# Transposing queries, keys and one-hot rows in larger groups, in a routed attention with a hard-swish FFN

## Chip, cores and metric

The kernel runs on one core of one Trainium2 chip. The metric is the device time of one execution in microseconds (us). Before the change it is 1071.25 us, the median of three runs (1070.79 to 1073.04 us). Engines are called as in the profile: PE is TensorE (PEld is its weight load), DVE is VectorE, ACT is ScalarE, POOL is GpSimd, SP is the engine that issues most DMA. L350 is line 350 of the kernel before.

## What is computed

First an attention in which a query may only look at keys of its own cluster, then a dense FFN. The reference, cut to what matters:

```python
# q, k, v: (4, 8, 768, 64); centroids: (8, 16, 64)
q_assign = np.argmax(np.einsum('bhsd,hcd->bhsc', q_n, c_n), axis=-1)     # q_n, k_n, c_n: unit rows
k_assign = np.argmax(np.einsum('bhsd,hcd->bhsc', k_n, c_n), axis=-1)
mask = q_assign[:, :, :, None] == k_assign[:, :, None, :]
scores = np.where(mask, scale * np.matmul(q, k.transpose(0, 1, 3, 2)), -1e9)
attn = softmax(scores)
x = np.matmul(attn, v)                      # regrouped to (3072, 512)
h = x @ w_in                                # 512 -> 2048
g = h * np.clip(h + 3.0, 0.0, 6.0) / 6.0
out = g @ w_out                             # 2048 -> 512
```

The kernel adds the mask by a second matmul into the same scores: a query's cluster as a one-hot row (1 at its cluster), a key's as the opposite row times a huge negative number (0 at its cluster, -2^60 at the others). Their product is 0 for the same cluster and -2^60 for another.

## The kernel before

Two heads are treated together as a pair; there are 16 pairs, g = 0 to 15. A pair has 12 chunks of 128 rows: 6 of queries (j = 0 to 5) and 6 of keys (j = 6 to 11). Each chunk holds both heads side by side. Before a pair's scores can run, its prep must be done; it is done while the pair before it runs its scores:

```python
NCH, NC2, NHC = 6, 12, 3          # chunks of queries, of both, half of NCH

def scratch(shape, name):         # a PSUM buffer for the prep
    if st["early"]:
        return psum_m.tile(shape, F32, name=name, tag="m")     # 2 buffers, shared with the FFN
    return psum_t.tile(shape, F32, name=name, tag="t")         # 1 buffer

def turn(g, part):                # queries and keys transposed: 4 parts of 3 chunks
    if part == 0:
        st["xf", g] = xp.tile([P, NC2, P], F32, name="xf")
    qk, xf = st["qk", g], st["xf", g]
    pt = scratch([P, NHC, P], "pqk")
    for i in range(NHC):
        j = part * NHC + i
        nc.tensor.transpose(out=pt[:, i], in_=qk[:, j // NCH, j % NCH], identity=ident)   # L294
    dst = xf[:, part * NHC : (part + 1) * NHC]
    nc.scalar.copy(out=dst, in_=pt)                                                       # L296

def cluster_scores(g): ...        # pcs: 4 matmuls of xf with the centroids, copied to cs by ACT
def route(g): ...                 # pr: 3 transposes of cs; DVE makes one_hot (bf16) from them

def route_turn(g, part):          # one-hot rows transposed by a matmul: 3 parts of 4 chunks
    if part == 0:
        st["xm", g] = xp.tile([P, NC2, P], BF16, name="xm")
    xm = st["xm", g]
    po = scratch([P, 4, P], "po")
    for i in range(4):
        j = part * 4 + i
        nc.tensor.matmul(                                                                 # L350
            po[:, i], lhsT=one_hot[:, j], rhs=(ident_q if j < NCH else ident_k),
            start=True, stop=True,
        )
    nc.scalar.copy(out=xm[:, part * 4 : part * 4 + 4], in_=po)                            # L354
```

`ident_k` is the identity times -2^60, so the matmul transposes and scales at once.

```python
def scores(n):                    # one of 12 blocks of a pair: key chunk j against half of the queries
    g, hf, j = where(n)
    scores_qk(n)                  # ps <- xf: key chunk 6 + j against 3 query chunks, both heads (L370)
    scores_part(n, st["xm", g], False)   # ps <- xm: the same with the one-hot rows, added (L370)
    ... ACT: ex = exp(ps)         # L382; ps has 2 buffers
    ... POOL: acc += ex           # L386, L389

def divide(n):                    # every 6 blocks
    pd = scratch([P, 512], "pd")
    ... PE: pd = sums of acc      # L420
    nc.vector.reciprocal(out=rcp, in_=pd)                                                 # L424
    ...

def prep_items(g, r):             # what of pair g's prep is done at which step
    if r in (0, 2):
        return [lambda: turn(g, r), lambda: turn(g, r + 1)]
    return {
        4: [lambda: cluster_scores(g)],
        6: [lambda: route(g)],
        8: [lambda: route_turn(g, 0), lambda: route_turn(g, 1)],
        10: [lambda: route_turn(g, 2)],
    }.get(r, [])

for n in range(0, total + lag_d + 2, 2):        # two blocks in each step; total = 192
    g, r = divmod(n, 12)
    scores(n); scores(n + 1)
    attn_v(n - 2); attn_v(n - 1)                # pv <- ex, vt (L399)
    if (n - 3) % 6 == 5: divide(n - 3)          # so at r = 2 and r = 8
    prep = prep_items(g + 1, r)
    if r == 4: prep.pop()()
    if n == 96: st["early"] = False             # from here on the scratch is the single buffer
    ...
    for i in range(max(len(prep), want)):       # want: how many FFN items this step takes
        if i < want: fill.pop(0)()              # an FFN item: 16 matmuls (ph, X or Y)
        if i < len(prep): prep[i]()
    ... some steps of weight decoding (DVE, ACT), until n = 96
```

In the steps up to n = 54 no FFN item runs, from n = 56 to 94 one in some of the steps, from n = 96 on mostly two or more. The engines execute in the order in which this loop records their instructions. Pair 0's prep runs before the loop (all parts in a row).

Of the kernel before, what the change touches and what calls it, by code (L numbers as in the profile page):

```python
# [8 lines left out]
F32 = mybir.dt.float32  # L9
BF16 = mybir.dt.bfloat16  # L10
# [3 lines left out]
ACT = mybir.ActivationFunctionType  # L14
# [4 lines left out]
P = 128  # L19
NCH = S // P  # L20
NC2 = 2 * NCH
HALF = S // 2
NHC = NCH // 2
# [17 lines left out]
FAR = 2.0**60  # L41
# [75 lines left out]
def fast_path(ctx, tc, ok, q, k, v, centroids, moe_w_in, moe_w_out, out):  # L117
# [3 lines left out]
    nc = tc.nc  # L121
    PSUM = bass.MemoryType.PSUM

    def pool(name, bufs, **kw):
        return ctx.enter_context(tc.tile_pool(name=name, bufs=bufs, **kw))

    const = pool("const", 1)
# [15 lines left out]
    psum_t = pool("psum_t", 1, space=PSUM)  # L143
    psum_m = pool("psum_m", 2, space=PSUM)
# [3 lines left out]
    g_sb = const.tile([P, 7, NFT // 2, P], F32, name="g_sb")  # L148
    ident = const.tile([P, P], F32, name="ident")
    ident_q = const.tile([P, P], BF16, name="ident_q")  # L150
    ident_k = const.tile([P, P], BF16, name="ident_k")
    ones = const.tile([P, D], F32, name="ones")
    half_c = const.tile([P, 1], F32, name="half_c")
    low_c = const.tile([P, 1], F32, name="low_c")
# [1 line left out]
    one_hot = const.tile([P, NC2, P], BF16, name="one_hot")  # L156
# [7 lines left out]
    st = {}  # L164
    later = []

    def scratch(shape, name):

        if st["early"]:
            return psum_m.tile(shape, F32, name=name, tag="m")  # L170
        return psum_t.tile(shape, F32, name=name, tag="t")

# [25 lines left out]
    def load_weights(i):  # L198
        if i < len(chunks):
            st["raw", i] = rawp.tile([P, WC, 2], U32, name="raw")  # L200
            nc.sync.dma_start(st["raw", i], chunks[i][1])
# [54 lines left out]
    def constants():  # L256
        make_identity(nc, ident)
        nc.vector.tensor_copy(out=ident_q, in_=ident)
        nc.vector.tensor_scalar_mul(out=ident_k, in0=ident, scalar1=-FAR)
        for t in range(2):  # L260
            nc.vector.tensor_reduce(
                out=parity[:, t : t + 1],
                in_=ident.rearrange("p (h t c) -> p t h c", t=2, c=C)[:, t], axis=AX.XY, op=ALU.max,
            )
        nc.gpsimd.memset(half_c, 0.5)
        nc.gpsimd.memset(low_c, 1.0 / BOUND)
        nc.gpsimd.memset(ones, 1.0)
        nc.gpsimd.memset(w_low, W_LOW)
        nc.gpsimd.memset(one_hot, 0.0)
# [17 lines left out]
    def turn(g, part):  # L287
        if part == 0:
            st["xf", g] = xp.tile([P, NC2, P], F32, name="xf")
        qk, xf = st["qk", g], st["xf", g]  # L290
        pt = scratch([P, NHC, P], "pqk")
        for i in range(NHC):
            j = part * NHC + i
            nc.tensor.transpose(out=pt[:, i], in_=qk[:, j // NCH, j % NCH], identity=ident)  # L294
        dst = xf[:, part * NHC : (part + 1) * NHC]
        nc.scalar.copy(out=dst, in_=pt)  # L296
        if part == 3:
            st.pop(("qk", g))


# [2 lines left out]
    def cluster_scores(g):  # L303
        c0, xf = (2 * g) % H * C, st["xf", g]
        ps = scratch([P, 512], "pcs")[:, 0 : NC2 // 4 * P]
        for a in range(4):
            nc.tensor.matmul(  # L307
                ps[a * 2 * C : (a + 1) * 2 * C], lhsT=cnT[:, c0 : c0 + 2 * C], rhs=xf[:, a::4],
                start=True, stop=True,
            )  # L310
        cs = st["cs", g] = rtp.tile([P, NC2 // 4, P], F32, name="cs")
        nc.scalar.copy(out=cs, in_=ps)
# [30 lines left out]
    def route_turn(g, part):  # L343
        if part == 0:
            st["xm", g] = xp.tile([P, NC2, P], BF16, name="xm")
        xm = st["xm", g]
        po = scratch([P, 4, P], "po")
        for i in range(4):
            j = part * 4 + i
            nc.tensor.matmul(  # L350
                po[:, i], lhsT=one_hot[:, j], rhs=(ident_q if j < NCH else ident_k),
                start=True, stop=True,
            )
        nc.scalar.copy(out=xm[:, part * 4 : part * 4 + 4], in_=po)  # L354


    def where(n):
# [3 lines left out]
    def scores_qk(n):  # L361
        g, hf, j = where(n)
        st["ps", n] = psum_s.tile([P, 2, 512], F32, name="ps")
        scores_part(n, st["xf", g], True)
# [179 lines left out]
    def prep_items(g, r):  # L544

        if g >= NPAIR:
            return []
        if r in (0, 2):
            return [lambda: turn(g, r), lambda: turn(g, r + 1)]
        return {  # L550
            4: [lambda: cluster_scores(g)],
            6: [lambda: route(g)],
            8: [lambda: route_turn(g, 0), lambda: route_turn(g, 1)],
            10: [lambda: route_turn(g, 2)],
        }.get(r, [])

    per_pair = 2 * NCH
# [30 lines left out]
    with tc.manual_schedule():  # L588
        nc.scalar.dma_start(cen, centroids.rearrange("h c d -> (h c) d"))
        load(0, "q", "k")  # L590
        constants()
        load(0, "v")
        load_weights(0)
        centroid_norm()
        for part in range(4):
            turn(0, part)
        load(1, "q", "k")
        scores_qk(0)
        scores_qk(1)
        cluster_scores(0)  # L600
        route(0)
        for part in range(3):
            route_turn(0, part)

        for n in range(0, total + lag_d + 2, 2):
            g, r = divmod(n, per_pair)
            for i in (n, n + 1):
                if i < total:
                    scores(i)
            for i in (n - lag_v, n - lag_v + 1):  # L610
                if 0 <= i < total:
                    attn_v(i)
            m = n - lag_d + 1
            if m >= 0 and m % NCH == NCH - 1:
                later.append(divide(m))
            prep = prep_items(g + 1, r)
            if r == 4 and prep:
                prep.pop()()
            if n == DECODED:
                st["early"] = False  # L620
            if m >= 0 and m % per_batch == per_batch - 1:
                fill += ffn_items(m // per_batch)
            if r == 6:
                load(g + 2, "q", "k")
                load(g + 1, "v")
            want = items_by(n + 2) - done if n < total else len(fill)
            want = min(want, len(fill))
            done += want
            for i in range(max(len(prep), want)):
                if i < want:  # L630
                    fill.pop(0)()
                if i < len(prep):
                    prep[i]()
            for step in decode[: share[r]]:
                step()
            del decode[: share[r]]
            for check in checks:
                check()
            checks, later[:] = later[:], []

        for check in checks:
            check()
# [384 lines left out]
```

## Time and profile before

| | |
|---|---|
| time, median of 3 | 1071.25 us |
| span of the profiled execution | 1069.7 us |
| PE busy | 97% of the span, 5490 matmul instructions |
| PEld busy | 68% |
| DVE, ACT, POOL busy | 43%, 37%, 29% |
| DMA queue of the loads, share of 16 engines | 15.0% |

The profile's second part shows the shares over time: DVE and ACT are at 7 to 9 tenths in the first quarter (while weights are decoded), and at 0 to 5 later; PE is at 9 tenths in all slices but the first and the last. "PE busy" counts the modelled time from a matmul's start to its end, and matmuls overlap: ten in a row, each of 0.22 us, take much less than 2.2 us. What one really takes of PE's time is seen in the distance from its start to the next one's in the timeline.

### The profile page before, as it was taken

To read this page: it belongs to the slowest core of one execution; us is meant where nothing else is said; L and a number is where in the kernel's file an instruction comes from. 1 tells how busy PE (TensorE), PEld (TensorE's weight loads), DVE (VectorE), ACT (ScalarE), POOL (GpSimd) and SP (SyncE) were. 2 spreads that over 40 slices of the span, in tenths; PEclk is the share of its full clock that TensorE was granted. 3 is DMA by queue.
4 is the path that set the end of the run, shared out by engine and by line. 5 is a ranking of instruction groups with operands and counts; after the bars stand their busy time and mean duration, and the time that the engine had idled before them with its cause. 6 is when DMAs were issued, how large, how long until landed. Compare 5 with 4: busy or idle time off the path is not lost.

```text
span 1069.7 us, 13428 instructions
## 1 busy us (share of the span) xinstructions
PE 1033.1 (97%) x5490; PEld 723.1 (68%) x5490; DVE 460.4 (43%) x658; ACT 392.3 (37%) x796; POOL 305.5 (29%) x171
## 2 busy tenths in 40 slices
PE   6999999999999999999999999999999999999997
PEld 3444454546888866667676766767676688888886
DVE  5799987688241331521342333152135132314141
ACT  5888876674121232342332333233233120201010
POOL 2777755554100023232232223222323200000000
PEclk9999999999999999999999999999999999999999
DMA  5444544330000201101020020200000000000000
GB/s 144 114 123 124 143 124 103 84 104 1 20 1 9 56 1 44 20 1 45 21 45 1 20 45 1 64 1 15 21 1 1 14 6 21 0 20 1 20 1 24
DMA packets 83543, 42.94 MB, mean 40 GB/s; under 512 B 76304, under 2 KB 76304, under 8 KB 83472
## 3 DMA queue, kind: packets, MB, share of 16 engines
q1 hardware_dynamic: 83328, 41.95, 15.0%
q8 instruction: 45, 0.74, 0.3%
q14 instruction: 26, 0.21, 0.1%
q10 hardware_dynamic: 144, 0.03, 0.0%
HBM read 35.68 MB, written 6.29 MB: 39 GB/s over the span
## 4 chain that ended last, share of the span: by engine, by line
PE 89%; ACT 5%; DVE 4%; issue 1%; POOL 0%; ACTq 0%; DVEq 0%; POOLq 0%
PE ph L476 31%; PE Y L494 16%; PE ps L370 14%; PE X L494 11%; PE pv L399 11%; PE pqk L294 2%; DVE g_sb L488 2%; PE pd L420 2%; PE po L350 1%; PE pcs L307 1%; DVE rcp L424 1%; ACT ex L382 1%; ACT xm L354 1%; ACT wsize L214 1%; ACT xf L296 1%
## 5 line engine op out<-in xcount | busy, mean ns | idle before, releaser
L389 POOL TENSOR_TENSOR acc<-acc,ex 128x768 f32<-128x768 f32 x128 | 244.3, 1909 | 368.5 <-ACT ex L382 362.9
L476 PE MATMUL ph<-xT,w_in_sb 128*128 128x256 f32 x1536 | 343.8, 381 | 0.0
L476 PEld LDWEIGHTS ph<-xT,w_in_sb 128*128 128x128 f32 x1536 | 287.8, 190 | 56.3 <-issue 10.2
L443 ACT ACTIVATE g_sb<-ph,half_c 128x512 f32<-128x512 f32 x96 | 66.0, 687 | 316.0 <-PE ph L476 316.0
L444 DVE SCALAR_TENSOR_TENSOR g_sb<-g_sb,ph 128x512 f32<-128x512 f32 x96 | 66.0, 687 | 254.8 <-ACT g_sb L443 254.8
L382 ACT ACTIVATE ex<-ps 128x768 f32<-128x768 f32 x192 | 148.4, 804 | 66.1 <-PE ps L370 65.8
L370 PE MATMUL ps<-xf 64*128 64x384 f32 x768 | 167.5, 515 | 1.2 <-ACT ex L382 0.8
L399 PE MATMUL pv<-ex,vt 128*64 128x384 f32 x768 | 145.6, 500 | 0.0
L424 DVE RECIPROCAL rcp<-pd 128x384 f32<-128x384 f32 x32 | 81.7, 2553 | 62.9 <-PE pd L420 61.8
L386 POOL TENSOR_TENSOR acc<-ex 128x768 f32<-128x768 f32 x32 | 59.0, 1843 | 173.2 <-ACT ex L382 173.2
L488 DVE TENSOR_TENSOR g_sb<-g_sb 128x256 f32<-128x256 f32 x192 | 103.7, 581 | 3.3
L399 PEld LDWEIGHTS pv<-ex,vt 128*64 128x64 f32 x768 | 46.7, 136 | 80.9 <-issue 77.0
L370 PEld LDWEIGHTS ps<-xf 64*128 64x128 f32 x768 | 63.9, 188 | 46.7 <-issue 32.2
L501 DVE TENSOR_TENSOR y<-y,Y 128x256 f32<-128x256 f32 x48 | 20.2, 421 | 171.4 <-PE Y L494 170.7
L494 PE MATMUL Y<-w_out_sb,g_sb 128*128 128x256 f32 x384 | 88.0, 382 | 0.0
L494 PE MATMUL X<-w_out_sb,g_sb 128*128 128x256 f32 x384 | 87.7, 381 | 0.0
L494 PE MATMUL Y<-T,g_sb 128*128 128x256 f32 x384 | 87.0, 380 | 0.0
L494 PEld LDWEIGHTS Y<-w_out_sb,g_sb 128*128 128x128 f32 x384 | 72.0, 190 | 16.5 <-issue 7.2
L494 PEld LDWEIGHTS X<-w_out_sb,g_sb 128*128 128x128 f32 x384 | 72.1, 190 | 14.2 <-issue 3.0
L494 PEld LDWEIGHTS Y<-T,g_sb 128*128 128x128 f32 x384 | 72.1, 190 | 9.3
L370 PE MATMUL ps<-xm 64*128 64x384 bf16 x384 | 63.8, 327 | 0.0
L296 ACT COPY xf<-pqk 128x384 f32<-128x384 f32 x64 | 30.0, 483 | 53.3 <-PE pqk L294 53.3
(83 smaller groups left out, 642.3 us busy)
## 6 DMA issues: line engine op xcount, KB each, us to landing
raw<-in_moe_w_in_dram SPq DMA_DIRECT2D x16, 512.0 KB, 3.8
raw<-in_moe_w_out_dram SPq DMA_DIRECT2D x16, 512.0 KB, 3.6
qk<-in_q_dram SPq DMA_DIRECT2D x32, 192.0 KB, 4.2
qk<-in_k_dram SPq DMA_DIRECT2D x32, 192.0 KB, 4.4
vt<-in_v_dram SPq DMA_DIRECT2D x32, 192.0 KB, 4.2
out_dram<-y SPq DMA_DIRECT2D x24, 256.0 KB, 2.2
cen<-in_centroids_dram ACTq DMA_DIRECT2D x1, 32.0 KB, 1.8
```

The costliest lines, as they stand in the source:

```text
L296: nc.scalar.copy(out=dst, in_=pt)
L370: nc.tensor.matmul(st["ps", n][:, t, 0:HALF], lhsT=x[r, NCH + j], rhs=x[r, hf * NHC : (hf + 1) * NHC], start=first, stop=not first,)
L382: nc.scalar.activation(out=ex, in_=sc, func=ACT.Exp, scale=SM_SCALE)
L386: nc.gpsimd.tensor_tensor(out=acc, in0=st["ex", n - 1], in1=ex, op=ALU.add)
L389: nc.gpsimd.tensor_tensor(out=acc, in0=acc, in1=ex, op=ALU.add)
L399: nc.tensor.matmul(pv[t * D : (t + 1) * D], lhsT=vt[:, j, t], rhs=ex[:, t], start=(j == 0), stop=(j == NCH - 1),)
L424: nc.vector.reciprocal(out=rcp, in_=pd)
L443: nc.scalar.activation(out=g, in_=h, func=ACT.Relu, bias=half_c, scale=1.0 / 6.0)
L444: nc.vector.scalar_tensor_tensor(out=g, in0=g, scalar=1.0, in1=h, op0=ALU.min, op1=ALU.mult)
L476: nc.tensor.matmul(ph[:, t * HC : (t + 1) * HC], lhsT=w_in_sb[:, kt, f * P : (f + 1) * P], rhs=xT[:, kt, 2 * m * P : 2 * (m + 1) * P], sta ...
L488: nc.vector.tensor_tensor(out=out_, in0=in0, in1=in1, op=op)
L494: nc.tensor.matmul(bank[:, half * HC : (half + 1) * HC], lhsT=g_sb[:, kind, i], rhs=w[:, i], start=(first and i == 0), stop=(last and i == ...
```

## The change

The prep's transpositions are grouped otherwise, and the one-hot rows are transposed in another way:

- Queries and keys are transposed in 3 parts of 4 chunks in place of 4 parts of 3. At r = 0 two parts are done (8 chunks), at r = 2 one (4 chunks).
- The one-hot rows are transposed in 2 parts of 6 chunks in place of 3 of 4: the queries' at r = 8, the keys' at r = 10. Six chunks of 128 elements fit one PSUM buffer because the result is bf16 now: it is a transposition proper (bf16 in, bf16 out) in place of a matmul with f32 result.
- The factor -2^60 of the keys' rows moves from the identity (`ident_k`, which goes) into ACT's copy out of PSUM.

It is meant to need fewer PSUM buffers, copies and waits per pair: 5 groups in place of 7. The diff, whole but for the hunks of the prologue's part counts (`range(4)` becomes `range(3)` for `turn`, `range(3)` becomes `range(2)` for `route_turn`):

```diff
-    ident_k = const.tile([P, P], BF16, name="ident_k")
...
-    def scratch(shape, name):
+    def scratch(shape, name, dtype=F32):
         if st["early"]:
-            return psum_m.tile(shape, F32, name=name, tag="m")
-        return psum_t.tile(shape, F32, name=name, tag="t")
+            return psum_m.tile(shape, dtype, name=name, tag="m")
+        return psum_t.tile(shape, dtype, name=name, tag="t")
...
-        nc.vector.tensor_scalar_mul(out=ident_k, in0=ident, scalar1=-FAR)
...
-        pt = scratch([P, NHC, P], "pqk")
-        for i in range(NHC):
-            j = part * NHC + i
+        pt = scratch([P, 4, P], "pqk")
+        for i in range(4):
+            j = part * 4 + i
             nc.tensor.transpose(out=pt[:, i], in_=qk[:, j // NCH, j % NCH], identity=ident)
-        dst = xf[:, part * NHC : (part + 1) * NHC]
+        dst = xf[:, part * 4 : part * 4 + 4]
         nc.scalar.copy(out=dst, in_=pt)
-        if part == 3:
+        if part == 2:
             st.pop(("qk", g))
...
-        po = scratch([P, 4, P], "po")
-        for i in range(4):
-            j = part * 4 + i
-            nc.tensor.matmul(
-                po[:, i], lhsT=one_hot[:, j], rhs=(ident_q if j < NCH else ident_k),
-                start=True, stop=True,
-            )
-        nc.scalar.copy(out=xm[:, part * 4 : part * 4 + 4], in_=po)
+        po = scratch([P, NCH, P], "po", BF16)
+        for i in range(NCH):
+            nc.tensor.transpose(out=po[:, i], in_=one_hot[:, part * NCH + i], identity=ident_q)
+        dst = xm[:, part * NCH : (part + 1) * NCH]
+        nc.scalar.activation(out=dst, in_=po, func=ACT.Copy, scale=-FAR if part else 1.0)
...
-        if r in (0, 2):
-            return [lambda: turn(g, r), lambda: turn(g, r + 1)]
         return {
+            0: [lambda: turn(g, 0), lambda: turn(g, 1)],
+            2: [lambda: turn(g, 2)],
             4: [lambda: cluster_scores(g)],
             6: [lambda: route(g)],
-            8: [lambda: route_turn(g, 0), lambda: route_turn(g, 1)],
-            10: [lambda: route_turn(g, 2)],
+            8: [lambda: route_turn(g, 0)],
+            10: [lambda: route_turn(g, 1)],
         }.get(r, [])
```

More of the change, by code (lines that the diff above doesn't have):

```diff
@@ L594, in fast_path @@
         centroid_norm()
-        for part in range(4):
+        for part in range(3):
             turn(0, part)
@@ L601, in fast_path @@
         route(0)
-        for part in range(3):
+        for part in range(2):
             route_turn(0, part)
```

## The prediction

> **What bounds the kernel now.** I read the page first (shares, slices, chain), then PE's waits, split at the step n = 96 (256.6 us), where the scratch goes from two buffers to one, then the timeline of PE and ACT in the steps that the change touches.
>
> ```profile
> PE 1033.1 (97%) x5490; PEld 723.1 (68%) x5490; DVE 460.4 (43%) x658; ACT 392.3 (37%) x796; POOL 305.5 (29%) x171
> ...
> PE 89%; ACT 5%; DVE 4%; issue 1%; POOL 0%; ACTq 0%; DVEq 0%; POOLq 0%
> ...
> L296 ACT COPY xf<-pqk 128x384 f32<-128x384 f32 x64 | 30.0, 483 | 53.3 <-PE pqk L294 53.3
> L354 ACT CAST xm<-po 128x512 bf16<-128x512 f32 x48 | 27.9, 584 | 39.9 <-PE po L350 39.5
> ```
>
> PE is the bound: 89% of the chain that ends last. Work taken from ACT or DVE counts only where PE waits for it, and such waits are few. PE's waits before 256.6 us, then after it:
>
> ```profile
> PE po L350 <- ACT xm L354: 6.3, 9, 1.0
> PE pqk L294 <- ACT xf L296: 6.1, 9, 0.8
> ```
>
> ```profile
> PE po L350 <- DVE rcp L424: 4.9, 4, 1.2
> PE po L350 <- ACT xm L354: 1.3, 2, 0.7
> PE pqk L294 <- ACT xf L296: 1.1, 2, 0.6
> ```
>
> The first pair of lines is what the change aims at: a second group of transpositions waits until ACT has copied the first out of the same scratch buffer. One step each of r = 8, r = 10 and r = 2, in PE's timeline:
>
> ```profile
> 74.81 0.55 PE L294 MATMUL pqk<-ident,qk 128*128 128x128 f32 x3
> 75.93 0.55 PE L294 MATMUL pqk<-ident,qk 128*128 128x128 f32 x3 [0.57 <-ACT xf L296]
> ...
> 88.47 0.40 PE L350 MATMUL po<-ident_q,one_hot 128*128 128x128 bf16 x4
> 89.54 0.27 PE L350 MATMUL po<-ident_q,one_hot 128*128 128x128 bf16 x2 [0.67 <-ACT xm L354]
> ...
> 93.11 0.40 PE L350 MATMUL po<-ident_k,one_hot 128*128 128x128 bf16 x4
> 93.44 0.92 PE L370 MATMUL ps<-xf 64*128 64x384 f32 x4
> 94.19 0.33 PE L370 MATMUL ps<-xm 64*128 64x384 bf16 x2
> ```
>
> Columns: start, length, engine and line, what, and in brackets the idle time before. At 93.11 four po matmuls and the block's edge take 0.33 us until the scores start. At 88.47 the next group starts 1.07 us later. Undisturbed, four need about 4 x 0.056 = 0.22 (0.40 us for four less the 0.219 of one is three distances, 0.06 each). So PE loses 0.84 us there, more than the 0.67 in the bracket, because the bracket counts from the modelled end of a matmul. At 74.81 likewise: 1.12 us less three distances of 0.11 (the first with 0.05 of edge) leaves 0.73.
>
> **What the Trainium skill says.** "TensorE: Matmul & The Clock Gate", Part 4 (PE-mode transpose): a bf16 128x128 transposition measures some 275 ns in a kernel's context, and does not count as activity for the clock. The trace of before shows durations of 273 ns for the f32 transpositions but a distance of 0.11 us, and 0.06 us for the bf16 matmuls; I take the distances, and 0.06 for bf16 transpositions too, which no run here shows yet. "PSUM — Partial Sum Buffer", Specifications: transposes write the input's dtype uncast, and ScalarE reads any dtype; so six bf16 chunks (1536 bytes) fit a 2 KiB bank. "ScalarE: Activation LUTs", What ACT_TABLE_LOAD costs: 0.833 ns per element for f32 and bf16 alike, plus a constant. The trace agrees for f32 sources: 483 ns for 384, 584 for 512, 804 for 768 elements (the exp). So a copy of 512 costs 584 and one of 768, bf16, about 800; that bf16 in PSUM is read no slower no run here shows. "TensorE: Matmul & The Clock Gate", Part 1: the clock halves after a window of 3.4 us with too little activity. The trace has such a stretch after the waits at 384 to 387 us:
>
> ```profile
> 386.00:393.00 7.00, 6.33 (x32) 3.02 (x32) 0.47 (x1) 3.56 (x8) 3.18 (x2) 0.76 0.01 4
> ```
>
> The 0.76 is the granted clock in these 7 us: 0.24 x 7.0 = 1.7 us lost.
>
> **The change, part by part.**
>
> *Second groups at r = 8 (removed).* Each of the 15 pairs in the loop had two po groups at r = 8; now there is one. Where no FFN item stands between the two, the wait goes: in the eight steps before 256.6 us, six at 0.84 us (as at 88.47) and two with an FFN item just ahead, whose gate keeps ACT busy (145.17 to 146.58 us: 1.41 - 0.22 = 1.19). That is 6 x 0.84 + 2 x 1.19 = 7.4. After 256.6 us the two that wait: 2 x 0.84 = 1.7. Sum -9.1 us. The other five late pairs have an FFN item between the groups and gain nothing.
>
> *Second group at r = 2 (removed).* The pairs prepared in steps 14 to 86 lose 0.73 to 0.98 each (0.73 three times in a quiet step, 0.83 and 0.82 at 102.8 and 129.2 us, 0.98 behind an FFN item, 0.73 once more): together -5.6 us. Nothing of this is there late, where FFN items separate the groups. One block's edge per step goes too: 7 x 0.05 = -0.4.
>
> *Moved work.* r = 0 gets two f32 transpositions more and r = 2 two less (0.22 us), r = 10 two bf16 ones more and r = 8 two less (0.11). Sum 0. The waits that stay at r = 0 (behind an FFN item at 192 and 227 us; at 475 and 736 us) are for a copy of 512 elements now, 0.1 longer: 4 x 0.1 = +0.4, in part covered by the fourth transposition.
>
> *The keys' rows come later (added).* This is the cost. Before, key chunks 6 and 7 came at r = 8 and were ready long before the next pair's first scores. Now all six come at r = 10, and the next pair's first scores need them in the very next PE work. From the start of the last po: 0.25 us until ACT can start (the last po starts at 89.71, its copy at 89.96), 0.80 for the copy, 0.05 for the signal, about 0.1 for the weight load of xm: 1.2 us. PE has until then one distance with edge (0.15) and four ps<-xf matmuls (94.19 - 93.44 = 0.75): 0.90. So at least 0.3 us of waiting. And ACT is not idle then:
>
> ```profile
> 92.00 1.49 ACT L382 ACTIVATE ex<-ps 128x768 f32<-128x768 f32 x2
> 93.55 0.59 ACT L354 CAST xm<-po 128x512 bf16<-128x512 f32 x1
> ```
>
> The copy starts right after the two exps, and with PE running ahead of ACT it will wait for them more. I put 0.4 to 0.9, on average 0.55, on each of the eight early r = 10 steps: +4.4 us. Late, an FFN item (3.5 us) lies between the keys' rows and the scores: 0.
>
> *Prologue.* Pair 0's two po groups and then the scores wait for two copies of 800 in a row (ACT starts at about 0.5 us of 1.6, ends 1.6 later): +0.7. One group of turns less: -0.1.
>
> *ACT and DVE give something back.* The steps from 40 to 120 us are full elsewhere too:
>
> ```profile
> 66.85:93.44 26.59, 25.03 (x163) 11.07 (x163) 24.43 (x29) 22.55 (x51) 19.71 (x11) 1.00 0.47 124
> ```
>
> Busy times of PE, PEld, DVE, ACT, POOL for one pair of 26.59 us: DVE 24.4, ACT 22.6. If PE's pair falls to 25.5, DVE has a little over 1 us of room for its 29 instructions and the small gaps between them, so it may lag, up to the slack of some 3 us between route (r = 6) and the first po (r = 8). ACT's work per pair falls only by 2 x 0.16. I put +1.0 on longer waits of ps for exp.
>
> *The clock at 387 us.* The wait for the reciprocal at 384.7 us (the four of 1.2 us in the list) is untouched: pd's buffer is the single scratch. But the second wait right after it (0.84) is gone, so I give the halved clock two chances in three to vanish: -1.1.
>
> Sum: -9.1 - 5.6 - 0.4 + 0.4 + 4.4 + 0.6 + 1.0 - 1.1 = -9.8 us; 1071.25 - 9.8 = about 1061 us, 1% faster.
>
> **The rivals.**
> *A new wait eats the gain.* The keys' copy on the path costs 1.5 us or more per early pair, because ACT lags by its exps and weight steps. For it: ACT's copy at 93.55 already starts at once after the exps. Against: over a pair ACT still has 3 us of room (25.5 less 22.6). It would make 8 x 1.5 = 12 of the 4.4: about 1068.
> *DVE becomes the bound in the first quarter.* For it: 24.4 of 26.6 us, and DVE's own waits are only 1.6 us between 40 and 120 us. Against: nobody waits for DVE there, and from 137 us on the FFN items give it room. It would take back up to 1 us for each of three or four pairs: about 1064.
> *bf16 transpositions or the bf16 read are slower than taken.* If a transposition took the 0.275 us of its duration, 192 x 0.22 = 42 us more, and about 1100. Against: the f32 transpositions pipeline at 0.11 us in spite of their 273 ns. I give it 1 in 50.
> *All waits vanish and ACT keeps up:* the added wait is 0.3 x 8 = 2.4, nothing given back: about 1057.
>
> **Range and chances.** 14.7 us of waits go for certain; what comes back is between 3 and 12 us. That gives 1056 to 1068 us for 8 in 10. 2% is 21 us, more than all that is removed (-9.1 - 5.6 - 0.4 - 1.7 = -16.8), so faster by over 2% has a chance of 0.01, slower by over 2% 0.02, within 2% 0.97.
>
> **What would show each step right or wrong.** In PE's waits, po on xm and pqk on xf should fall from 7.7 and 7.2 us to about 0 and 2.5; po on the reciprocal should stay at 4.9. A new line, ps (or PEld) on xm, should show eight times, 0.2 to 0.9 each. The bf16 transpositions should stand 0.06 us apart, the xm copies take 0.80 us, 32 in number, the xf copies 0.58, 48 in number. The clock should be 1.0 around 387 us. The prediction is wrong if that new line is over 8 us, if waits on exp grow by several us, or if the transpositions run at another pace.

## The result, and the profile after

The kernel after the change takes 1060.65 us, the median of its runs (1059.82 to 1062.58), and the kernel before takes 1071.29 us beside it: a ratio of 0.990, with a 95% interval of 0.9882 to 0.9919. That is 10.6 us less, close to the 1061.0 predicted. The single terms were less good than their sum, as will be seen.

The kernel's lines have moved: L292 and L294 are now the transpositions of queries and keys and their copy, L347 and L349 those of the one-hot rows, L365 the scores, L377 the exp, L415 and L419 the sums and the reciprocal. First the shares of the engines and the chain that ends last:

```profile
PE 1027.9 (97%) x5490; PEld 720.2 (68%) x5490; DVE 472.6 (45%) x657; ACT 388.5 (37%) x764; POOL 303.8 (29%) x171
...
PE 86%; DVE 7%; ACT 5%; issue 1%; DMA 0%; POOL 0%; ACTq 0%; DVEq 0%; POOLq 0%
```

PE is the bound as before. ACT has 32 instructions less (796 to 764) and loses only 3.8 us of work; DVE does one instruction less and is busy 12 us *longer*. This oddity will come back. The groups of instructions, with different shapes kept apart (count, then total and mean ns of one):

```profile
L294 ACT COPY xf<-pqk 128x512 f32<-128x512 f32 x48 | 27.6, 590 | 37.1 <-PE pqk L292 36.7
L349 ACT ACTIVATE xm<-po 128x768 bf16<-128x768 bf16 x32 | 25.8, 808 | 34.7 <-PE po L347 34.7
L347 PE MATMUL po<-ident_q,one_hot 128*128 128x128 bf16 x192 | 15.9, 220 | 6.7 <-DVE rcp L419 5.0 <-DVE one_hot L325 1.7
```

48 copies of 590 ns and 32 of 808 ns: the counts and durations that the prediction took. PE's waits over the whole span (total us, times, longest):

```profile
PE po L347 <- DVE rcp L419: 5.0, 4, 1.2
PE ps L365 <- ACT ex L377: 3.3, 7, 0.9
PE pqk L292 <- ACT xf L294: 3.0, 4, 0.8
PE ps L365 <- ACT xm L349: 2.7, 5, 1.3
PE po L347 <- DVE one_hot L325: 1.7, 2, 1.1
```

The waits of po for xm (7.7 us) are gone, those of pqk for xf fell from 7.2 to 3.0. Two kinds of wait matter now that did not before: ps waits for xm (the keys' rows come late) and ps waits for ex. One pair's r = 0 and the ends of its r = 8 and r = 10, with the starts of the steps behind them, in PE's timeline:

```profile
63.29 0.92 PE L365 MATMUL ps<-xf 64*128 64x384 f32 x4 [0.23 <-ACT ex L377]
64.70 0.34 PE L365 MATMUL ps<-xm 64*128 64x384 bf16 x2 [0.49 <-ACT xm L349]
...
84.79 0.51 PE L347 MATMUL po<-ident_q,one_hot 128*128 128x128 bf16 x6
85.22 0.92 PE L365 MATMUL ps<-xf 64*128 64x384 f32 x4
85.97 0.33 PE L365 MATMUL ps<-xm 64*128 64x384 bf16 x2
...
88.48 0.51 PE L347 MATMUL po<-ident_q,one_hot 128*128 128x128 bf16 x6
88.92 0.92 PE L365 MATMUL ps<-xf 64*128 64x384 f32 x4
89.89 0.34 PE L365 MATMUL ps<-xm 64*128 64x384 bf16 x2
```

At 84.79 six transpositions and the block's edge take 0.43 us to the next start: (0.51 - 0.22) / 5 = 0.058 us from one to the next. At 64.70 the first scores of a pair wait 0.49 us for the keys' rows. At 89.89 they wait too, though no bracket says so: ps<-xm starts 0.97 us after its ps<-xf, and 0.75 us at 85.97, where nothing is late. The brackets count idle time from the modelled end of a matmul and miss such a wait of 0.22 us. So the list has only four of the eight waits on xm in the loop (its fifth, of 1.3 us, is the prologue's), and the lengths of steps, below, show all eight.

To say where the 10.6 us come from, the document uses one measure throughout: a *step's length*, from the start of its first ps<-xf matmul to that of the next step's, read from PE's timeline. Such lengths repeat within some 0.01 us between the traces in most steps, so single waits can be told although the times of one kernel's runs spread by up to 4 us. There are two exceptions: a few early steps in which PE waits for exps (n = 36, 50 and 54, below), and the first 25 us. There the granted clock is halved for 0 to 7 us, differently from trace to trace whatever the kernel, which is worth up to 3 us. The trace of before has such a stretch at the start, from 15.9 to 19.3 us, and the trace of after has none; so the spans of the two traces (1069.7 and 1058.0) differ by 1 us more than the medians.

| steps, after less before | us | of it work moved |
|---|---|---|
| before PE's first matmul | -0.4 | |
| prologue and step n = 0 (with the clock) | -0.9 | +0.2 |
| r = 2 (15 steps) | -8.2 | -3.3 |
| r = 8 (15 steps) | -9.9 | -1.7 |
| r = 0 (14 steps) | +6.6 | +3.1 |
| r = 10 (15 steps) | +0.2 | +1.7 |
| r = 6 | +0.7 | |

The steps of r = 4 are unchanged. r = 10 has +1.7 from moved transpositions and -1.6 from one step, n = 106, in which the clock is no longer halved. The windows' row for the place after the reciprocal's wait (busy us of PE, PEld, DVE, ACT, POOL, then the granted clock):

```profile
377.00:384.00 7.00, 6.84 (x41) 4.46 (x41) 0.66 (x2) 3.00 (x7) 3.62 (x2) 1.00 0.01 2
```

Before, a stretch of the same place had 0.76.

### The profile page after: what moved, and what is told of

It is laid out like the page before. It is cut to its first block, busy times and chain, and to the rows that moved or that the text cites. A ratio compares the mean times of both kernels' runs of the same rounds, so it can differ in the third digit from the quotient of the medians.

```text
span 1058.0 us, 13396 instructions
## 1 busy us (share of the span) xinstructions
PE 1027.9 (97%) x5490; PEld 720.2 (68%) x5490; DVE 472.6 (45%) x657; ACT 388.5 (37%) x764; POOL 303.8 (29%) x171
## 4 chain that ended last, share of the span: by engine, by line
PE 86%; DVE 7%; ACT 5%; issue 1%; DMA 0%; POOL 0%; ACTq 0%; DVEq 0%; POOLq 0%
PE ph L471 31%; PE Y L489 16%; PE ps L365 12%; PE X L489 11%; PE pv L394 10%; PE pqk L292 2%; DVE g_sb L483 2%; DVE rcp L419 2%; PE pd L415 1%; ACT ex L377 1%; PE pcs L305 1%; ACT xm L349 1%; PE po L347 1%; ACT wsize L213 1%; DVE wunit L239 1%
## 5 line engine op out<-in xcount | busy, mean ns | idle before, releaser
L377 ACT ACTIVATE ex<-ps 128x768 f32<-128x768 f32 x192 | 148.0, 804 | 78.1 <-PE ps L365 78.1
L365 PE MATMUL ps<-xf 64*128 64x384 f32 x768 | 166.1, 511 | 3.4 <-ACT ex L377 3.3
L483 DVE TENSOR_TENSOR g_sb<-g_sb 128x256 f32<-128x256 f32 x192 | 113.5, 632 | 3.2
L419 DVE RECIPROCAL rcp<-pd 128x384 f32<-128x384 f32 x32 | 81.7, 2552 | 60.9 <-PE pd L415 59.7
L365 PEld LDWEIGHTS ps<-xf 64*128 64x128 f32 x768 | 63.6, 187 | 49.0 <-issue 33.2
L365 PE MATMUL ps<-xm 64*128 64x384 bf16 x384 | 63.1, 323 | 3.0 <-ACT xm L349 2.7
L489 PE MATMUL X<-T,g_sb 128*128 128x256 f32 x192 | 44.0, 382 | 0.0
```

The costliest lines, as they stand in the source:

```text
L365: nc.tensor.matmul(st["ps", n][:, t, 0:HALF], lhsT=x[r, NCH + j], rhs=x[r, hf * NHC : (hf + 1) * NHC], start=first, stop=not first,)
L377: nc.scalar.activation(out=ex, in_=sc, func=ACT.Exp, scale=SM_SCALE)
L483: nc.vector.tensor_tensor(out=out_, in0=in0, in1=in1, op=op)
L489: nc.tensor.matmul(bank[:, half * HC : (half + 1) * HC], lhsT=g_sb[:, kind, i], rhs=w[:, i], start=(first and i == 0), stop=(last and i == ...
```

## The experiments

All ratios are to the kernel before, beside runs of it on the same chip.

**Each part alone.** `t_only` groups queries and keys in 3 parts of 4 and leaves the one-hot rows as before; `o_only` does the opposite.

```diff
 # t_only                                       # o_only
-  pt = scratch([P, NHC, P], "pqk")             (turn as before: 4 parts of 3)
+  pt = scratch([P, 4, P], "pqk")               +  po = scratch([P, NCH, P], "po", BF16)
   (route_turn as before: 3 parts of 4)         +  nc.tensor.transpose(out=po[:, i], ...)
```

> Only the queries and keys are regrouped (3 parts of 4 chunks); the one-hot rows stay 3 f32 groups of 4. If the waits at r = 2 are the cost of the seven parts as predicted (-5.6 us, -0.4 of edges, +0.4 of longer copies at r = 0), the time falls by 5 to 6 us to about 1065.5, and po's waits on xm stay at 7.7 us. Rival, that the transpositions of q and k are hidden and all of the gain is the one-hot rows': within 1 us of 1071.3.

> Only the one-hot rows are changed (2 bf16 groups of 6, factor in the copy); queries and keys stay 4 parts of 3. Predicted parts: -9.1 us at r = 8, +3 to 4.4 us for the keys' rows on the path at r = 0, -1.1 to -1.7 for the halved clock at 387 us if it goes: about 1064, 6 to 8 us less. If DVE is what sets the pace in the first quarter, the two halves of the change alone gain more together (over 12 us) than the whole change (10.6 us); if every wait is independent, they add up to 10.6 within 1 us.

Measured: t_only 1065.2 us (0.9949, 0.9933 to 0.9965), o_only 1066.83 us (0.9962, 0.9949 to 0.9975). The gains are 6.3 and 4.7 us, 11.0 together, against 10.6 for both at once: within what these medians can tell, the parts add. Their waits, PE's of t_only:

```profile
PE po L350 <- ACT xm L354: 7.9, 11, 1.0
PE pqk L294 <- ACT xf L296: 3.0, 4, 0.8
```

and PE's of o_only:

```profile
PE pqk L292 <- ACT xf L294: 8.2, 11, 1.6
PE ps L365 <- ACT xm L349: 2.6, 6, 1.0
PE ps L365 <- ACT ex L377: 1.3, 5, 0.3
```

Each part removes its own wait and leaves the other's. (In o_only that of pqk for xf is 1.0 us more than the 7.2 of before: one wait, at n = 14, takes 1.56 us, since ACT waited 0.96 us for a load of weights ahead of the copy.) The late keys' rows (ps on xm) come with the one-hot part alone. In the steps, t_only gives the early r = 2 steps -7.7 us (of it 1.8 moved) and o_only the early r = 8 steps -8.3 (0.9 moved). In after the same sums are only -6.7 and -7.4. So each part gains 0.8 to 1.0 us more in these steps alone than with the other: a first sign of something given back.

**bf16 transpositions, without regrouping.** `bf16_3x4` is the kernel before with the one-hot rows transposed as bf16 and scaled in the copy, but still in 3 parts of 4 chunks.

```diff
-  po = scratch([P, 4, P], "po")
+  po = scratch([P, 4, P], "po", BF16)
-  nc.tensor.matmul(po[:, i], lhsT=one_hot[:, j], rhs=(ident_q if j < NCH else ident_k), ...)
+  nc.tensor.transpose(out=po[:, i], in_=one_hot[:, j], identity=ident_q)
-  nc.scalar.copy(out=xm[:, part * 4 : part * 4 + 4], in_=po)
+  # part 1 holds 2 chunks of queries and 2 of keys: two copies, with scale 1 and -FAR
+  for a, b in ((0, 4),) if part != 1 else ((0, 2), (2, 4)):
+      nc.scalar.activation(out=xm[...], in_=po[:, a:b], func=ACT.Copy, scale=...)
```

> Only the kind of transposition is changed: bf16 transpositions and the factor in the copy, but 3 groups of 4 as before (the mixed group in two copies of 256). If bf16 transpositions cost PE the same 0.056 us as the matmuls and only the grouping brings the gain, the time stays at 1071.3 within 1.5 us, with po waits a little longer (two short copies in place of one, some 0.1 us). If the other kind of transposition itself brings some of the gain, it is below 1069.

Measured: 1071.05 us (0.9999, 0.9992 to 1.0007), no difference. The groups by shape:

```profile
L349 ACT ACTIVATE xm<-po 128x512 bf16<-128x512 bf16 x32 | 19.0, 595 | 34.4 <-PE po L347 34.2
L347 PE MATMUL po<-ident_q,one_hot 128*128 128x128 bf16 x192 | 18.5, 219 | 14.1 <-ACT xm L349 8.0 <-DVE rcp L422 5.0 <-DVE one_hot L325 1.1
```

595 ns for 512 elements of bf16 where the f32 ones took 584, and 219 ns for a transposition where the matmul took 219: the new operations cost what the old ones did. The wait on xm stays at 8.0 us. The form of the transposition is worth nothing by itself; what it brings is that six chunks fit one buffer. In the steps, the early r = 8 ones stand within 0.012 us of before.

**The keys' rows earlier, first way.** If the late rows at r = 0 are to be blamed on their place in PE's program, putting them before attn_v in the same step (r = 10) should help: 1.5 us more of PE work then lies between them and the scores.

```diff
 # hoist10
   scores(n); scores(n + 1)
+  prep = prep_items(g + 1, r)
+  if r in (10,) and prep: prep.pop(0)()
   attn_v(n - 2); attn_v(n - 1)
```

> The changed kernel with the keys' one-hot rows transposed right after the scores of step r = 10, ahead of attn_v, so that 1.44 us of pv matmuls lie between them and the scores that need them. If the wait of ps on xm (3.0 us in eight steps by the changed kernel's trace) is what the later keys' rows cost, it goes and the time falls by 2 to 3 us, to about 1058. If ACT or DVE sets the pace there anyway, the wait only moves to ps on exp, and the time stays within 1 us of 1060.6.

Measured: 1061.58 us (0.9906, 0.989 to 0.9921): not better than after. PE's timeline and then ACT's, of hoist10:

```profile
63.70 0.33 PE L365 MATMUL ps<-xm 64*128 64x384 bf16 x2
63.96 0.51 PE L347 MATMUL po<-ident_q,one_hot 128*128 128x128 bf16 x6
64.40 1.51 PE L394 MATMUL pv<-ex,vt 128*64 128x384 f32 x8
66.15 0.92 PE L365 MATMUL ps<-xf 64*128 64x384 f32 x4 [0.24 <-ACT ex L377]
67.55 0.34 PE L365 MATMUL ps<-xm 64*128 64x384 bf16 x2 [0.49 <-ACT xm L349]
```

```profile
65.31 1.49 ACT L377 ACTIVATE ex<-ps 128x768 f32<-128x768 f32 x2
66.69 0.81 ACT L349 ACTIVATE xm<-po 128x768 bf16<-128x768 bf16 x1
```

The transpositions are done by 64.5 us, but the copy starts at 66.69: ACT does first the two exps that stand before it in its program. These do not wait for their scores, whose last matmuls ended at 63.70 + 0.33 = 64.03. ACT is behind: it works on parts of the weight decoding and of the routing until it reaches the exps at 65.31, with no idle time before them. So the 0.49 us at 67.55 is the very 0.49 of after's 64.70, and no r = 0 step before n = 96 loses more than 0.11 us of its wait for the rows (n = 96 loses all of its 0.47). The early wait is set by ACT's order and backlog, not by PE's place for the transpositions.

**The keys' rows earlier, second way.** `hoist10_mid` puts them between the two blocks of score matmuls of the step, so that the copy stands ahead of the second exp in ACT's program.

```diff
 # hoist10_mid: in the loop that records scores(n) and scores(n + 1)
+  if i == n and r == 10 and n < DECODED and prep: prep.pop(0)()
```

> The changed kernel with the keys' rows of r = 10 transposed between the two score blocks of the step (until n = 94), so that their copy stands ahead of the second exp in ScalarE's order. With them after both blocks the wait stayed, so the theory is now that it is not TensorE's order but ScalarE's: the copy stands behind two exps that wait their turn. Then one exp less (0.7 us) ahead of the copy takes away the 0.2 us waits of four pairs and the 0.65 us waits of two, 2 to 2.5 us in all by the steps' sums. If the wait moves to ps on exp again, nothing is gained.

Measured: 1061.98 us (0.9919, 0.9905 to 0.9932), no better. PE's waits:

```profile
PE ps L365 <- ACT ex L377: 3.7, 7, 1.2
PE ps L365 <- ACT xm L349: 1.3, 1, 1.3
```

The wait for xm in the loop is gone (the 1.3 is the prologue's). At r = 0 the early steps shorten by 0.23 (three of them), 0.35, and 0.81 where a wait for an exp goes with it (0.58 of it, at n = 36; more on that step below); the two other ones keep all but 0.07. The step n = 96 gains 0.47. Against it, six of the eight early r = 10 steps lengthen, by 0.20 (three), 0.39 (two, with an FFN item) and 0.31: the block of score matmuls is cut in two for the transpositions. What is gained at r = 0 (2.5 us, 1.9 without the exp's 0.58) is lost there (1.7) and in part in new waits at n = 50 and 54 (0.5).

**The keys' rows at r = 8 again.** `both8` keeps the groups of six but does both at r = 8, the second behind the first.

```diff
-            8: [lambda: route_turn(g, 0)],
-            10: [lambda: route_turn(g, 1)],
+            8: [lambda: route_turn(g, 0), lambda: route_turn(g, 1)],
```

> The changed kernel with both one-hot groups of 6 at r = 8, none at r = 10: the keys' rows are early again, and the second group waits for the first one's copy again. By the steps' sums: +1.4 us at r = 8 in each of the eight pairs before n = 96 (a wait of 1.06 and six transpositions), -0.44 at r = 10 and -0.2 to -0.65 at r = 0 each, +1.05 in the two late steps without an FFN item between: about +6 to +7 us, near 1067. If the later keys' rows cost more than the wait of ps on xm shows (through ScalarE's and VectorE's backlog), it is less: below 1064.

Measured: 1068.08 us (0.9972, 0.9963 to 0.9981), 7.4 us above after. PE's timeline:

```profile
87.54 0.51 PE L347 MATMUL po<-ident_q,one_hot 128*128 128x128 bf16 x6
88.95 0.49 PE L347 MATMUL po<-ident_q,one_hot 128*128 128x128 bf16 x6 [0.90 <-ACT xm L349]
89.38 0.92 PE L365 MATMUL ps<-xf 64*128 64x384 f32 x4
```

Against after, six of the eight early r = 8 steps lengthen by 1.39 us and the other two by 1.47 and 1.64; with 0.44 of transpositions and edge moved in from r = 10, the wait is 0.95. In return r = 0 is shorter by 0.23 (four steps), 0.35, 0.66 (two) and 0.47 at n = 96; n = 36, one of the four, gains another 0.58 that belongs to an exp. That is the direct measure of what the late keys' rows cost: 4 x 0.23 + 0.35 + 2 x 0.66 + 0.47 = 3.1 us. It is a third of what the change gains at r = 8.

**Is the give-back a lag of DVE?** In after, PE waits for exps at 124.87 and 133.61 us, which before did not happen. ACT's timeline just ahead of the first:

```profile
122.50 0.68 ACT L213 ACTIVATE wsize<-raw 128x512 bf16<-128x512 f32 x1 [1.10 <-DMA raw<-in_moe_w_out_dram]
124.03 1.49 ACT L377 ACTIVATE ex<-ps 128x768 f32<-128x768 f32 x2
```

and PE's, in after:

```profile
124.87 0.92 PE L365 MATMUL ps<-xf 64*128 64x384 f32 x4 [0.82 <-ACT ex L377]
133.61 0.92 PE L365 MATMUL ps<-xf 64*128 64x384 f32 x4 [0.90 <-ACT ex L377]
```

ACT waits 1.10 us for a load of weights, and the exps behind it are late. The load is late because its buffer was: `raw` has two buffers, and the loads of the queue wait for the DVE step (wunit) that frees one. From 34 to 142 us ACT waits 6.6 us for such loads in after, and 0.7 in before. A third buffer would take away the link, without touching anything else:

```diff
 # after_raw3 (from after), before_raw3 (from before)
-    rawp = decoding.enter_context(tc.tile_pool(name="rawp", bufs=2))
+    rawp = decoding.enter_context(tc.tile_pool(name="rawp", bufs=3))
```

> The changed kernel with three buffers in place of two for the raw weights. Theory: in the fourth and fifth pair (about 90 to 135 us) VectorE has fallen behind, frees the raw weights late, their load starts late, ScalarE waits for it (6.6 us in eight waits between 34 and 142 us) with the exps behind it, and TensorE waits for the exps (0.6, 0.9 and 0.7 us at the steps n = 36, 50 and 54). A third buffer breaks that chain: these three waits go and the time falls by about 2 us, to 1058.5. Rival: VectorE is the bound itself there; the waits move to the one-hot rows and the reciprocal, and the time stays within 1 us of 1060.6.

> The kernel before with three raw weight buffers. There VectorE keeps up (1.6 us of its own waits between 40 and 120 us) and ScalarE waits 0.7 us for the raw weights, so the third buffer should do nothing: within 1 us of 1071. If it gains 1 us or more as in the changed kernel, the buffer's gain has nothing to do with the change.

Measured: after_raw3 1059.45 us (0.9902, 0.9887 to 0.9917), before_raw3 1071.47 us (0.9994, 0.9985 to 1.0003). On the medians alone after_raw3 cannot be told from after, but its steps can. PE's waits from 84 to 142 us, in after:

```profile
PE ps L365 <- ACT ex L377: 2.2, 3, 0.9
PE po L347 <- DVE one_hot L325: 0.6, 1, 0.6
```

and in after_raw3:

```profile
PE ps L365 <- ACT ex L377: 0.6, 1, 0.6
PE po L347 <- DVE one_hot L325: 0.6, 1, 0.6
```

With the third buffer, ACT's waits for raw are gone from that stretch; the steps n = 14, 36, 50 and 54 shorten by 0.14, 0.58, 0.89 and 0.29 us, and n = 56 lengthens by 0.16. In before the third buffer changes no early step after the first 25 us by more than 0.02 us.

The 0.58 of n = 36 can't be credited to the buffer. `hoist_where`, further down, has two buffers and is the same program as after up to n = 70: a second trace of it, but for a clock halved for nearly 7 us at the start. There n = 36 takes 4.51 us, as with three buffers (5.09 in after), while n = 50 and 54 wait 1.15 and 0.95 us in place of 0.89 and 0.72. So where the lag strikes differs from trace to trace. What the third buffer takes away is 1.2 us of after's trace without n = 36, and 1.6 us between hoist_where and the same with three buffers.

So the link is this: PE's shorter pair leaves DVE no room, DVE frees raw late, the load lands late, ACT stands still, the exps are late, PE waits. Two more runs agree. In both8, also with two buffers, PE is held up at r = 8, and n = 50 and 54 do not wait (4.49 and 3.97 us, as in t_only, which has no waits there). In o_only, with a shorter pair than before, the link shows once, at n = 14. The wait for one_hot and 0.4 us at n = 54 stay with three buffers.

**Groups ahead of attn_v elsewhere.** Two waits remain in after: po for the reciprocal, 5.0 us in four steps of r = 8 behind `divide`, and pqk for xf, 3.0 us in four of r = 0. In `hoist_0_8`, the first group of r = 0 (always) and that of r = 8 (in the late steps) goes ahead of attn_v: the pv matmuls then lie between it and the next user of the scratch. `hoist_three` is that with the edit of hoist10_mid.

```diff
 # hoist_0_8
   scores(n); scores(n + 1)
+  prep = prep_items(g + 1, r)
+  if (r == 0 or r == 8 and n > DECODED) and prep: prep.pop(0)()
   attn_v(n - 2); attn_v(n - 1)
```

> The changed kernel with two other groups moved ahead of attn_v and the row sums: the first group of q and k at r = 0 (all pairs) and the queries' one-hot rows at r = 8 (after n = 96). The second group of q and k then finds its buffer copied (four waits left, 0.84 to 0.98 each: -3.6 us), and the one-hot group no longer waits for the reciprocal that holds the single scratch buffer (four steps of 1.4 to 1.5 us, 5.0 in PE's waits: -5.6 us). Together 8 to 9 us less than the changed kernel, about 1052. If one_hot comes too late from VectorE for the earlier place, or the row sums then wait for the one-hot copy, half of it or less.

> Both of the last two edits together. If their waits are independent, the sum of their gains: about 10 us less than the changed kernel, about 1050.5.

Measured: hoist_0_8 1057.32 us (0.988, 0.9865 to 0.9895), hoist_three 1058.65 us (0.9893, 0.9878 to 0.9908). Both waits are gone: the four r = 8 steps gain 1.20 or 1.25 us each, the four r = 0 steps 0.74 to 0.89. But most of the other steps, in which a group was hoisted without a wait to save, lose 0.15 us, the price of the group's new place; and two steps, n = 134 and 146, lose 1.45 us. PE's timeline at the second of them, and then DVE's, both of hoist_0_8:

```profile
536.33 0.66 PE L292 MATMUL pqk<-ident,qk 128*128 128x128 f32 x4 [1.23 <-DVE rcp L419]
```

```profile
529.02 4.78 DVE L483 TENSOR_TENSOR g_sb<-g_sb 128x256 f32<-128x256 f32 x4
533.73 2.54 DVE L419 RECIPROCAL rcp<-pd 128x384 f32<-128x384 f32 x1
```

DVE's four sums and differences of the FFN took 4.78 us here, while POOL's additions ran from 529.60 to 533.52 us. In after the same four took 3.18 us (next fence), with POOL's additions from 533.87 us on. So in hoist_0_8 the reciprocal behind them came late against PE, and with it the scratch that the next group needs.

```profile
532.85 3.18 DVE L483 TENSOR_TENSOR g_sb<-g_sb 128x256 f32<-128x256 f32 x4
535.95 2.55 DVE L419 RECIPROCAL rcp<-pd 128x384 f32<-128x384 f32 x1
```

So hoist_0_8 gains 3.3 us against after on the medians, not the 8 to 9 expected. hoist_three adds what hoist10_mid had shown, 0.2 us at r = 10 for what r = 0 gains, and one more new wait: at n = 94 an FFN item waits 1.13 us for a reciprocal. The gains of the two edits do not add.

**Only where a wait was.** `hoist_where` hoists only in the steps whose wait was seen: r = 0 where exactly one FFN item runs, and r = 8 in the pairs with g % 4 below 2 late. `hoist_where_raw3` has the third raw buffer too.

```diff
 # hoist_where
+  prep = prep_items(g + 1, r)
+  one = n < total and min(items_by(n + 2) - done, len(fill)) == 1
+  if (r == 0 and one or r == 8 and n > DECODED and g % 4 < 2) and prep: prep.pop(0)()
```

> The changed kernel, with a group moved ahead of attn_v only where a wait stood: at r = 0 in the four steps with exactly one FFN item, at r = 8 in the four late steps in which the one-hot group waited for the reciprocal. By the steps' sums of the run with all of them moved: -0.87, -0.89, -0.74, -0.74 at r = 0 and -1.20, -1.25, -1.20, -1.25 at r = 8, without the new waits at r = 2 (1.45 twice) and the 0.15 of block edges elsewhere: about -8 us against the changed kernel, 1052.5 to 1053.

> The same with three raw weight buffers: another 1 to 1.5 us, if the two are independent; about 1051.5, 1.8% below the kernel before.

Measured: hoist_where 1053.25 us (0.983, 0.9813 to 0.9846), hoist_where_raw3 1051.22 us (0.9814, 0.9801 to 0.9827). Against after, the r = 8 steps give 2 x 1.20 + 2 x 1.25 = 4.9 us and the r = 0 steps 0.88 + 0.88 + 0.74 + 0.74 = 3.2 us; no other late step changes. Of the early ones n = 36 lacks its 0.58 and a few others move by up to 0.27; up to n = 70 the program is that of after, so this is no effect of the edit. PE's timeline at the first of the r = 8 steps:

```profile
371.31 0.51 PE L347 MATMUL po<-ident_q,one_hot 128*128 128x128 bf16 x6
371.75 1.51 PE L394 MATMUL pv<-ex,vt 128*64 128x384 f32 x8
373.13 0.87 PE L415 MATMUL pd<-acc,ones 128*64 128x384 f32 x4
```

The group comes before the sums of the divide in the single scratch, and its copy is done while pv runs. The third raw buffer is worth 1.6 us in the steps after the first 25 us; between the two medians are 2.0 us, which their intervals alone do not tell apart. Both beat the kernel before and the kernel after.

## Why the prediction was right, and where not

*The bound and the chain.* Right: PE sets the time, and 32 copies fewer on ACT gained nothing where PE had not waited: the late r = 8 steps without a wait shorten by the moved 0.11 us alone. The waits were what counted.

*Second groups at r = 8 and r = 2 (-9.1 and -6.0).* Right, in mechanism and size. In quiet steps r = 8 shortens by 0.945 us, that is 0.84 of wait and 0.11 of moved work, and behind an FFN item by 1.30 and 1.13. r = 2 shortens by 1.007 us, 0.22 of it moved. Leaving the moved work and the new waits aside, the sums are -8.9 and -6.0 us. That each part removes its own waits without the other was shown by t_only and o_only; most of what is given back (below) comes only with both.

*The cost of the operations.* Right: 0.058 us from one bf16 transposition to the next, copies of 590 and 808 ns; that the new kind costs what the old one did, bf16_3x4 shows apart from the regrouping (219 ns, and 595 ns for 512 elements). The rival of slow transpositions or reads is out. bf16 in PSUM is read no slower than f32: 808 less 595 ns over 256 elements is 0.832 ns each, the rate that the prediction had taken.

*Moved work (0).* Right to 0.01 us in the quiet steps. Of the four longer copies (+0.4), the two late steps that can be read apart from other changes show 0.1 each.

*The keys' rows come later (+4.4).* Mis-sized, and only half explained: 3.1 us, as both8 shows. The prediction put 0.4 to 0.9 on each step, 0.55 on average; measured are 0.23 four times, 0.35, 0.47 and 0.66 twice. The lower bound, "at least 0.3", was too high by 0.07. The reason it gave, ACT behind with its exps, is what hoist10 shows: moving PE's part 1.5 us earlier changed the early waits by 0.11 us at most, since the copy stands behind two exps in ACT's program and these behind ACT's other work. Why the eight waits differ in size was not isolated. The rival of a new wait that eats the gain (1.5 us or more per pair) is out: the largest in the loop is 0.7.

*ACT and DVE give something back (+1.0).* This is the term that was mis-sized: 3.2 us. It consists of 0.58 (n = 36), 0.89 (n = 50), 0.72 (n = 54) of waits for exps, 0.67 at n = 44 for one_hot, and 0.34 in smaller pieces. The prediction had seen that DVE would have little over 1 us of room in a pair of 25.5 us, and took PE's slack of 3 us between route and the first po as what DVE would lag into. That slack, read from before as the time from the end of one_hot to the first po, is 2.4 to 3.0 us in three of the eight early pairs and 6.1 in two, but 1.9 in two and 1.3 in the pair of n = 42 and 44. There the lag shows directly. DVE's maximum of the cluster scores, from which one_hot is made, in before and then in after:

```profile
112.42 0.55 DVE L321 TENSOR_REDUCE mx<-pr 128x24 f32<-128x384 f32 x1
```

```profile
109.59 0.55 DVE L319 TENSOR_REDUCE mx<-pr 128x24 f32<-128x384 f32 x1
```

It starts 5.14 us after the step n = 42 in before and 7.05 us after it in after, behind weight steps that follow each other with gaps of at most 0.04 us; one_hot is 1.9 us later, more than the slack, and PE waits. t_only, alone, has the same wait (0.71 us), o_only has none. DVE was nearly full: over the steps n = 12 to 52 it is idle for 5.7 of 93.7 us in before and for 4.2 of 91.3 in after, such gaps included. (In the slices of before DVE stands at 9 tenths from 53 to 134 us; over the first quarter it ranges from 5 to 9 and ACT from 4 to 8, and not from 7 to 9.)

The prediction did not see the other way from DVE to PE: through the two raw buffers to the weights' loads, and from there to ACT and its exps, which have no such slack. The third buffer shows this link for 1.2 of the 3.2 us; for n = 36 the chain is the same in after's trace (ACT waits 0.57 us for raw ahead of it), but no run isolates it. Some of DVE's operations become longer too, as the last section shows, but in these early steps others become shorter (xT's +1.6 us with one operation less, wunit's -0.9), so how much that adds to the lag is open. The rival in which DVE becomes the bound was half right, for four steps.

*Prologue (+0.6).* Half right. Against bf16_3x4, whose first matmul starts at the same time and whose clock is not halved there either, the step n = 2 of after begins 0.66 us later, of which 0.22 is moved work: 0.44 us, a little less than said. But PE's first matmul now starts at 5.98 us and not at 6.39: making ident_k took an operation on DVE at the very start, ahead of the work PE waits for. That term, -0.4 us, was missed in the diff.

*The clock at 387 us (-1.1).* The mechanism fits the traces, and the size is 1.6 us in the one seen: n = 106 is 1.53 us shorter though it holds 0.11 us more work. There are two such places in each kernel, at r = 8 of n = 104 and 152, where po waits 1.24 us for the reciprocal. In the five kernels in which a second wait of 0.67 to 0.90 us followed (before, before_raw3, bf16_3x4, t_only, both8), 6 of the 10 places were followed by a halved stretch of 3.4 us. In the traces of the kernels that have the first wait alone (after, o_only, hoist10, after_raw3, hoist10_mid), none of 10. "TensorE: Matmul & The Clock Gate", Part 1, of the Trainium skill gives windows of about 3.4 us in which activity is counted; that fits the length of the stretches. It puts the return to the halved clock after at least one idle window of that length; here it took less, for no wait at these places is longer than 1.24 us. 1.24 us alone never did it, and with the second wait, together some 1.9 to 2.1 us, it happened in 6 of 10. Where a window begins can't be seen, so why 4 of the 10 escaped stays open.

*The sum.* The terms as measured are -8.9 - 6.0 + 0.2 + 3.1 + 3.2 - 1.6 + 0.4 - 0.4 = -10.0. With 0.15 us less each at n = 36 and 48, which t_only shows too and no step of the prediction held, that is -10.3; the medians say -10.6. The prediction of -9.8 was this close by luck, because errors offset: 1.3 us too much for the keys' rows and 1.1 too little gained on the clock, in the prologue and at the start, against 2.2 too little for the give-back.

*Open.* What makes up the 0.4 us at n = 54 that stay with three buffers was not tried. Why two r = 0 steps of hoist10_mid keep their length, and why the wait at n = 36 stands in one of two traces of the same early program, was not isolated either.

## What to carry to other kernels

A second group that waits for the copy of the first costs the copy and two hand-overs, here 0.7 to 0.95 us in quiet steps, so fewer and larger groups pay on the bound engine even when the work is the same. A copy is only as early as its place in its own engine's program: moving the producer ahead helps little when the consumer stands behind other work. Where an engine with no slack gets a shorter period, follow what it frees (here a load buffer) to the engine that works behind it, and try one buffer more; and reorder only the steps whose wait was seen, as an extra cut in a row of matmuls had a price here, 0.15 to 0.39 us in most steps.

## What the runs showed of the hardware

*DVE's two-input operations stretch beside POOL's.* The group of xT, the product of num and rcp, in before (total us, mean ns):

```profile
L425 DVE TENSOR_TENSOR xT<-num,rcp 128x384 f32<-128x384 f32 x32 | 20.4, 638 | 2.3
```

and in after:

```profile
L420 DVE TENSOR_TENSOR xT<-num,rcp 128x384 f32<-128x384 f32 x32 | 27.0, 845 | 2.3
```

The same 32 operations, unchanged in the program, took 207 ns longer on average: one at 114.69 us, wholly beside POOL's additions (114.58 to 118.48), took 2.11 us, and one at 538.53 us, after POOL had ended at 537.70, took 0.56. The reciprocals, with one input, and that in PSUM, stayed at 2553 and 2552 ns. The Trainium skill's "SBUF — State Buffer", Who interferes with whom, says that a DVE operation with two inputs in SBUF contends with POOL's reads; the numbers here agree with it. Of the 12 us that DVE is busier in after, xT makes 6.6, and the FFN's sums and differences, also of two inputs, 9.8 (192 of them, 103.7 us before and 113.5 after); its other work takes some 4 us less. The 1.6 us of hoist_0_8's sums (4.78 in place of 3.18) have the same look. That an engine with the same program becomes slower because its operations now meet POOL's at other times is what these numbers suggest; no run took POOL's additions away to prove it.

*A cut in a block of matmuls costs.* Placing a group of transpositions where it saves no wait lengthened the step by 0.15 us (hoist_0_8) and, between two score blocks, by 0.20 to 0.39 (hoist10_mid), with no matmul more. It is not the same everywhere: in hoist10 the late r = 10 steps grew by 0.05 us.
